# A three-stage attention and mixing kernel: weight ring in two parts, weight conversions moved into token mixing, two factors split

## The chip, the cores and the metric

One core of a Trainium2 chip. The metric is the device time of one execution in microseconds, the median of several runs. The names TensorE (PE, with its weight loads PEld), VectorE (DVE), ScalarE (ACT), GpSimd (POOL) and SyncE (SP) are used as in the profile.

## The reference, cut to what matters

Three layers on 4 batches of 576 positions and 512 features, all float32:

```python
# attention with feature maps (8 heads of 64), then
u = x + real(fft(fft(x, axis=1), axis=2))          # layer 1
u = u + relu(layernorm(u) @ w_ch1) @ w_ch2         # 512 -> 2048 -> 512
h = relu(u.transpose(0, 2, 1) @ w_tok1) @ w_tok2   # layer 2: 576 -> 256 -> 576
u = u + h.transpose(0, 2, 1)                       # token mixing
out = u + relu(u @ w_ch1) @ w_ch2                  # channel mixing: 512 -> 1536 -> 512
```

## The kernel before, in words

Every product of float32 matrices is made of three matmuls of rounded parts (high times high, high times low, low times high). A high part is a ScalarE cast, a low part the difference, on VectorE or GpSimd.

The last layer is what the change touches. *Token mixing* takes the batches in the order 2, 3, 0, 1. Per batch there are five steps: `c_tr` transposes 128 positions on TensorE, ScalarE casts the result (`yth`, L1060), VectorE subtracts (`ytl`, L1061), and `c_tok1` multiplies (L1074 to L1076). Then come `hh` and `hl` (L1081, L1082), `c_tok2` (L1094) in two halves of four sums, and VectorE adds these to `u` (L1100).

*Channel mixing* is 24 units (p, b): six slices p of the hidden width for batches 2 and 3 in turn, then for 0 and 1. A unit multiplies 2 by 2 blocks with seven products in place of eight, twice: seven first products of 6 matmuls (L876) from the prepared factors `x` of `x_prep` (L845 to L852) into the banks X, Y, Z, and seven second products of 6 matmuls (L885), from the factors `g` of `part` (L911, low part through `later`, whose line is L1319). Their inputs are the four `relu` results and sums of these (`sums1` L919, L920; `sums2` L926). Factors 5 and 7 are made as a pair, and 6 and 4 as a pair. `flush` adds each finished sum to `u` (L940); in a batch's last unit it writes `outT` instead (L935, stores L938 on SP's queue). Second products of a unit run beside first products of the next.

The weights of channel mixing are needed as rounded parts of the seven factors. `w_seven` makes one quarter of those of a slice (p, which, s): raw words come in (L624), `words2` makes floats of them (ScalarE L509, VectorE L512, L513, L515, some microseconds later), GpSimd makes four sums of blocks (L644), ScalarE the high part (L652), GpSimd the low part in two pieces (L656), and both go to a scratch in DRAM (L663). `wa_plain` does the same for the token weights. `w_load` brings the parts of one slice back (L676, `ring`, three slots of 1792 KB), one load for the first products and one for the second of every pair of units.

The order of the work is written out by hand: `at(t, fn)` and `later(dt, fn)` put a call into a heap ordered by a planned time, and instructions are emitted in that order; each engine and each queue runs its instructions in order. `te` is the planned end of layer 1, `td` the planned start of channel mixing (69 behind it), and a unit has TU = 11.15 of planned time:

```python
second_ = ((20, x1), (21, z7), (23, x6), (24, z4), (26, x5), (30, y2), (31, x3))   # in TU/14
late = ahead[18:24]                                   # six conversions
at(td - 16 + 15 * n, w_seven, p, which, s, True)      # n = 0 to 5, first operation 12 later
```

The other 27 conversions run in layer 1, one every 9.3.

Of the kernel before, what the change touches and what calls it, by code (L numbers as in the profile page):

```python
# [46 lines left out]
HB = 288  # L47
# [7 lines left out]
def mixer_kernel(ctx: ExitStack, tc: tile.TileContext, qT, kT, vt, wphi, w11, w12, wt1, wt2, w21, w22,  # L55
# [73 lines left out]
    def a_open():  # L129
        ones = st.tile([128, 128], F32, name="ones")  # L130
        nc.vector.memset(ones, 1.0 / D)
        T["ones"] = ones
        T["ones_r"] = st.tile([128, 128], F32R, name="ones_r")
# [9 lines left out]
        P["tmp"] = pool("tmp", 1, "right")  # L143
# [469 lines left out]
    def w_seven(p, which, s, late=False):  # L613
# [25 lines left out]
        def then(v):  # L639
            a11, a12, a22, a21 = (v[:, n * 128:(n + 1) * 128] for n in range(4))  # L640
            x = [N["x"][:, n * 128:(n + 1) * 128] for n in range(4)]
            for o, a, c, op in ((0, a21, a22, ALU.add), (1, x[0], a11, ALU.subtract), (2, a11, a21, ALU.subtract),
                                (3, a12, x[1], ALU.subtract)):
                nc.gpsimd.tensor_tensor(out=x[o], in0=a, in1=c, op=op)  # L644
# [26 lines left out]
    def w_load(which, p, v):  # L671
# [154 lines left out]
    WI = {1: 4, 2: 5, 4: 6, 5: 0, 6: 1, 7: 2, 3: 3}  # L826
# [37 lines left out]
    def unit(p, b, v, last, t0, tu, end=False):  # L864
# [5 lines left out]
        def prod(i, out, start, stop):  # L870
            w, x = W2[0, v], T["xx", b]
            need(("xx", b, XI[i]))
            k = 0
            for kk in range(2):
                for hw, hx in ((0, 0), (0, 1), (1, 0)):
                    nc.tensor.matmul(out, w[:, kk, hw, WI[i]], x[XI[i]][:, hx, kk], start=(start and k == 0),  # L876
                                     stop=(stop and k == 5), skip_group_check=(i != 2))
                    k += 1

        def prod2(i, o, start, stop):  # L880
            w, g = W2[1, v], G[i]
# [83 lines left out]
        def s_x3():  # L965
# [50 lines left out]
        def y2():  # L1016
            if not end:
                open_z("y")
                return second(2, "y", True, True, 0, 0)
            o = [pw()[:, 0:HB] for _ in range(2)]  # L1020
            prod2(2, o, True, True)
            for m in range(2):
                later(0.3, flush, o[m].unsqueeze(1), 0, 0, (m,))
# [11 lines left out]
    def c_open():  # L1035
# [10 lines left out]
        T["ytl"] = pc.tile([128, 4, 512], F32R, name="ytl")  # L1046
# [3 lines left out]
    def c_tr(b, kt):  # L1050
# [4 lines left out]
        h = P["cv"].tile([128, 512, 2], F32R, tag="raw", name="yth", bufs=2).rearrange("q c t -> q (c t)")[:, 0:512]  # L1055
        l = T["ytl"][:, kt % 4]
# [250 lines left out]
    for n, (_, p, which, s) in enumerate(late):  # L1307
        at(td - 16 + 15 * n, w_seven, p, which, s, True)
# [69 lines left out]
```

## Time and profile before

| what | value |
|---|---|
| median of 3 runs | 1083.12 us (1082.85 to 1086.86) |
| profiled execution | 1085.0 us |
| its span | 1083.3 us, mean granted clock 0.991 |
| TensorE busy | 1030.6 us (95%) |
| VectorE, ScalarE, GpSimd busy | 711.2, 442.2, 460.1 us |
| attention and layer 1 | 0 to 692.6 us |
| token mixing | 692.6 to 764.9 us |
| channel mixing | 764.9 to 1083.3 us |

The profile is of one execution. Its span begins with the first instruction and ends with the last; 1.7 us of the execution's time lie around it. Stages are told apart by the lines that TensorE works on. Line numbers are those of the kernel before; in the changed kernel the same lines stand 3 to 7 further down.

### The profile page before, as it was taken

Reading aid. Unit: us, or ns where it says so; the run is one execution under the profiler, and the core shown is the slowest. Engines: PE = TensorE matmul, PEld = TensorE weight load, DVE = VectorE, ACT = ScalarE, POOL = GpSimd, SP = SyncE. Lnnn points to the kernel's source line nnn. Section 1 sums busy time; section 2 is a strip of 40 time slices with the busy share of each in tenths; the row PEclk is TensorE's granted clock in tenths of the full one; section 3 lists DMA queues with packets and bytes.
Section 4 is the critical chain, followed back from the end, with each engine's and each line's share of the span. In section 5 each row is a group of like instructions: output and inputs, shape, how many; then the busy total and the mean of one; then the engine's idle time right before and its main releaser. Section 6 shows DMA issues by size and latency. Waiting matters only on the chain.

```text
span 1083.3 us, 19688 instructions
## 1 busy us (share of the span) xinstructions
PE 1030.6 (95%) x7596; PEld 951.3 (88%) x7596; DVE 711.2 (66%) x1265; ACT 442.2 (41%) x961; POOL 460.1 (42%) x451
## 2 busy tenths in 40 slices
PE   9999999999999989999999999999788899899996
PEld 9887787867899989999999999987788799799995
DVE  5799787999756786634676333354567677756666
ACT  5776556653223433322333121134444435444441
POOL 3464334322102344443444000045767758656551
PEclk9999999999999999999999999999999999999999
DMA  5575564462057543675733363800255544545332
GB/s 183 172 217 178 162 200 168 141 224 84 12 221 232 183 151 108 228 265 192 282 127 134 121 216 119 333 2 27 84 191 215 196 156 148 201 160 192 136 137 88
DMA packets 63785, 178.41 MB, mean 165 GB/s; under 512 B 8660, under 2 KB 30100, under 8 KB 57036
## 3 DMA queue, kind: packets, MB, share of 16 engines
q1 hardware_dynamic: 55628, 143.60, 38.6%
q10 hardware_dynamic: 8064, 33.56, 8.2%
q8 instruction: 60, 0.98, 0.4%
q14 instruction: 33, 0.27, 0.1%
HBM read 126.39 MB, written 48.31 MB: 161 GB/s over the span
## 4 chain that ended last, share of the span: by engine, by line
PE 56%; DVE 9%; POOL 5%; issue 3%; ACT 1%; DMA 1%; ACTq 0%; DVEq 0%; POOLq 0%
PE pw L790 16%; PE pz L885 9%; PE pw L876 8%; POOL g L1319 3%; PE pk L813 3%; PE pk L812 3%; PE pk L814 3%; PE pa L812 3%; PE pa L814 3%; PE pa L813 3%; PE pw L1094 1%; PE pa L1094 1%; DVE t L513 1%; PE pk L1075 1%; DVE t L512 1%
## 5 line engine op out<-in xcount | busy, mean ns | idle before, releaser
L790 PE MATMUL pw<-xh,w 128*128 128x288 f32 x896 | 197.5, 295 | 0.0
L885 PE MATMUL pz<-g,ring 128*128 128x288 f32 x1002 | 157.6, 301 | 19.5 <-POOL g L1319 9.8
L885 PEld LDWEIGHTS pz<-g,ring 128*128 128x128 f32 x1002 | 141.4, 191 | 25.9 <-POOL g L1319 14.5
L876 PE MATMUL pw<-x,ring 128*128 128x288 f32 x1008 | 153.4, 299 | 10.3 <-DVE f L898 5.4
L798 DVE SCALAR_TENSOR_TENSOR gl<-pw,gh 128x288 fp32r<-128x288 f32 x128 | 58.0, 454 | 148.8 <-ACT gh L797 148.5
L876 PEld LDWEIGHTS pw<-x,ring 128*128 128x128 f32 x1008 | 140.8, 190 | 13.2 <-DVE f L898 7.0
L790 PEld LDWEIGHTS pw<-xh,w 128*128 128x128 f32 x896 | 149.9, 188 | 1.2 <-issue 1.0
L940 DVE TENSOR_TENSOR u<-u,pz 128x576 f32<-128x576 f32 x152 | 113.9, 752 | 56.4 <-PE pz L885 52.9
L797 ACT ACTIVATE gh<-pw 128x288 fp32r<-128x288 f32 x128 | 52.6, 411 | 213.6 <-PE pw L790 211.8
L790 PE MATMUL pw<-xl,w 128*128 128x288 f32 x448 | 132.3, 295 | 0.5 <-POOL xl L773 0.5
L199 POOL TENSOR_TENSOR l<-raw,h 128x384 fp32r<-128x384 f32 x48 | 51.8, 1084 | 96.2 <-ACT h L195 83.7
L1319 POOL TENSOR_TENSOR g<-t,g 128x576 fp32r<-128x576 f32 x46 | 66.3, 1442 | 52.4 <-ACT g L911 49.6
L790 PEld LDWEIGHTS pw<-xl,w 128*128 128x128 f32 x448 | 84.1, 188 | 0.7 <-POOL xl L773 0.7
L812 PE MATMUL pk<-gh,w 128*128 128x288 f32 x256 | 76.4, 298 | 4.7 <-ACT gh L797 2.8
L813 PE MATMUL pk<-gl,w 128*128 128x288 f32 x256 | 76.8, 300 | 4.1 <-DVE gl L798 4.1
L812 PE MATMUL pa<-gh,w 128*128 128x288 f32 x256 | 75.9, 297 | 0.0
L814 PE MATMUL pk<-gh,w 128*128 128x288 f32 x256 | 75.8, 296 | 0.0
L814 PE MATMUL pa<-gh,w 128*128 128x288 f32 x256 | 75.6, 295 | 0.0
L813 PE MATMUL pa<-gl,w 128*128 128x288 f32 x256 | 75.4, 294 | 0.0
L1319 ACT ACTIVATE f<-f 128x288 f32<-128x288 f32 x72 | 32.0, 444 | 90.3 <-DVE f L898 90.1
L1319 POOL TENSOR_TENSOR g<-f,g 128x288 fp32r<-128x288 f32 x69 | 58.1, 856 | 20.4 <-ACT g L911 20.2
L259 PEld LDWEIGHTS pk<-v,ek 128*128 128x128 f32 x512 | 61.6, 192 | 5.8 <-issue 5.8
(205 smaller groups left out, 2385.0 us busy)
## 6 DMA issues: line engine op xcount, KB each, us to landing
ring<-wd SPq DMA_DIRECT2D x24, 1792.0 KB
w<-wd ACTq DMA_DIRECT2D x24, 1024.0 KB
raw<-in_w SPq DMA_DIRECT2D x32, 512.0 KB
wd<-wst SPq DMA_DIRECT2D x24, 448.0 KB
wd<-raw SPq DMA_DIRECT2D x24, 448.0 KB
wd<-wst SPq DMA_DIRECT2D x16, 512.0 KB
wd<-w ACTq DMA_DIRECT2D x32, 256.0 KB
raw<-in_w SPq DMA_DIRECT2D x48, 128.0 KB
```

The source lines that it names most:

```text
L199: nc.gpsimd.tensor_tensor(out=l, in0=src, in1=h, op=ALU.subtract)
L259: nc.tensor.matmul(T["kv", i][j][:, o:o + 65], e[:, (t % 2) * 2 + j, s, :], v[:, t - 1, j * 65:j * 65 + 65], start=False, stop=(u == 1 and ...
L790: nc.tensor.matmul(out, w[:, k, fs], x[:, k, :], start=(n == 0), stop=(n == 11))
L797: nc.scalar.activation(out=gh, in_=out, func=AF.Relu)
L798: nc.vector.scalar_tensor_tensor(out=gl, in0=out, scalar=0.0, in1=gh, op0=ALU.max, op1=ALU.subtract)
L812: nc.tensor.matmul(out, wh[:, f % 4, ds], gh, start=(f == f0), stop=False)
L813: nc.tensor.matmul(out, wh[:, f % 4, ds], gl, start=False, stop=False)
L814: nc.tensor.matmul(out, wl[:, f % 4, ds], gh, start=False, stop=last)
L876: nc.tensor.matmul(out, w[:, kk, hw, WI[i]], x[XI[i]][:, hx, kk], start=(start and k == 0), stop=(stop and k == 5), skip_group_check=(i != 2))
L885: nc.tensor.matmul(o[s], w[:, s, hw, WI[i]], g[hx], start=(start and k == 0), stop=(stop and k == 2), skip_group_check=(i != 2))
L940: nc.vector.tensor_tensor(out=u, in0=u, in1=o, op=ALU.add)
L1319: fn(*a, **k)
```

## The change

- `yth` gets four slots of its own in the pool of token mixing, where it shared two buffers `raw` with the conversions. `ones` and `ones_r` move to another pool.
- The four sums of a conversion are written to other slots, in an order that fits (L644). The parts of a slice lie in the order in which factors are used (`WI`).
- `w_load` makes two parts of every load: part 0 with the four factors that are used first, part 1 with the other three, in two DMAs as these lie at both ends of the row. Each part has three slots of its own and its own planned time.
- 24 conversions (15 of channel weights and the 9 of token weights, mixed) run in layer 1, one every 9.0. The last nine begin 36 before its planned end, one every 13: two meet the end of layer 1, five token mixing, two the first two units.
- The pair (6, 4) becomes two factors: 6 is made 3.4 after its last first product, 4 at the old place. The pair (5, 7) comes 0.2 earlier. Second products run in the order x1, z7, x6, x5, z4, x3, y2.
- In the last unit the sums of x go to two banks of the pool `pw`, flushed one by one, and y2 to a bank of `pz`.

```diff
     def w_load(which, p, v):   # now (which, p, v, part, eng)
-        t = P["r"].tile([128, 2, 2, 7, 128], F32R, tag="w", name="ring", bufs=3)
-        W2[which, v] = t
-        nc.sync.dma_start(out=t.bitcast(F32), in_=WD[1, which, p])
+        i0 = 2 - which
+        n = (4, 3)[part]
+        t = P["r"].tile([128, 2, 2, n, 128], F32R, tag="w%d" % part, name="ring", bufs=3)
+        src = WD[1, which, p]
+        for o, a, e in ((0, i0, i0 + 4),) if part == 0 else ((0, 0, i0), (i0, i0 + 4, 7)):
+            eng.dma_start(out=t[:, :, :, o:o + e - a].bitcast(F32), in_=src[:, :, :, a:e])
+            for k in range(a, e):
+                W2[which, v, k] = t[:, :, :, o + k - a]
...
-    WI = {1: 4, 2: 5, 4: 6, 5: 0, 6: 1, 7: 2, 3: 3}
+    WI = {3: 0, 5: 1, 6: 2, 7: 3, 1: 4, 2: 5, 4: 6}
...
-            ga = P["g"].tile([128, 2, n, HB], F32R, tag="g%d" % n, name="g", bufs=5 if n == 1 else 3)
+            ga = P["g"].tile([128, 2, n, HB], F32R, tag="g%d" % n, name="g", bufs=6 if n == 1 else 2)
...
-            later(2.2 if end else 2.8, lambda: part((5, 7), h["t13"], 2))
-            if end:
-                later(2.7, lambda: part(6, h["t24"][:, 0:1]))
+            later(2.2 if end else 2.6, lambda: part((5, 7), h["t13"], 2))
+            later(2.7 if end else 3.4, lambda: part(6, h["t24"][:, 0:1]))
...
-            later(4.2, lambda: part((6, 4), h["t24"], 2))
+            later(4.2, lambda: part(4, h["t24"][:, 1:2]))
...
         def open_x():
-            h["x"] = pz()
+            h["x"] = [pw()[:, 0:HB] for _ in range(2)] if end else pz()
...
             o = h[key]
+            if isinstance(o, list):
+                prod2(i, o, start, stop)
+                for m in range(2):
+                    later(0.3, flush, o[m].unsqueeze(1), row, hf, (m,))
+                return
...
-        second_ = ((20, x1), (21, z7), (23, x6), (24, z4), (26, x5), (30, y2), (31, x3))
+        second_ = ((20, x1), (21, z7), (23, x6), (26, x5), (28.2, z4), (30, x3), (31.5, y2))
...
-        h = P["cv"].tile([128, 512, 2], F32R, tag="raw", name="yth", bufs=2).rearrange("q c t -> q (c t)")[:, 0:512]
-        l = T["ytl"][:, kt % 4]
+        h, l = T["yth"][:, kt % 4], T["ytl"][:, kt % 4]
...
-    late = ahead[18:24]
-    del ahead[18:24]
-    tcv = tb2 - V('c2', 40)
+    sevens, plain = ahead[:24], ahead[24:]
+    lanes = [(plain if n % 8 in (2, 5, 7) else sevens).pop(0) for n in range(24)]
+    tcv = tb2 - V('c2', 38)
...
-        tcv += V('c4', 9.3)
+        tcv += V('c4', 9.0)
+    tcv = max(tcv, te - 36)
+    for kind, *a in sevens:
+        at(tcv, w_seven, *a, True)
+        tcv += 13
...
-                t = times1[n] - 2 * TU + (0.2 * TU + 0.5 if which == 0 else 1.1 * TU + 0.5)
-                at(tc_ + 0.3 + 0.01 * (2 * v + which) if 2 * v + which < 3 else t + TU, w_load, which, p, v)
+                for part, t in enumerate((-1.05, -0.65) if which == 0 else (-0.5, 0.1)):
...
+                        at(times1[n] + t * TU, w_load, which, p, v, part, nc.sync)
...
-    for n, (_, p, which, s) in enumerate(late):
-        at(td - 16 + 15 * n, w_seven, p, which, s, True)
```

VectorE at the start of token mixing, first before and then changed (`gl` and the sums from `pk`, `pa` are the end of layer 1; L1061, L1082 and L1100 are `ytl`, `hl` and the sums, L1064, L1085 and L1103 in the changed kernel):

```order
L1061 TENSOR_TENSOR ytl<-pw,yth 128x512
L817 TENSOR_TENSOR u<-u,pk 128x288 x2
L817 TENSOR_TENSOR u<-u,pa 128x288 x2
L1061 TENSOR_TENSOR ytl<-pw,yth 128x512 x2
L1061 TENSOR_TENSOR ytl<-pw,yth 64x512
L1082 SCALAR_TENSOR_TENSOR hl<-pk,hh 128x512 x2
L1061 TENSOR_TENSOR ytl<-pw,yth 128x512 x2
L1100 TENSOR_TENSOR u<-u,pw 128x288
```

```order
L1064 TENSOR_TENSOR ytl<-pw,yth 128x512
L822 TENSOR_TENSOR u<-u,pk 128x288 x2
L822 TENSOR_TENSOR u<-u,pa 128x288 x2
L512 TENSOR_SCALAR t<-t 128x512
L513 SCALAR_TENSOR_TENSOR t<-raw,t 128x512
L515 SCALAR_TENSOR_TENSOR t<-raw,t 128x512
L1064 TENSOR_TENSOR ytl<-pw,yth 128x512 x2
L1064 TENSOR_TENSOR ytl<-pw,yth 64x512
L1085 SCALAR_TENSOR_TENSOR hl<-pk,hh 128x512 x2
L1064 TENSOR_TENSOR ytl<-pw,yth 128x512 x2
L512 TENSOR_SCALAR t<-t 128x512
L513 SCALAR_TENSOR_TENSOR t<-raw,t 128x512
```

The bit operations of two conversions now stand among the first batch's and the second batch's operations; three more follow in the later batches.

GpSimd in unit 0, first before and then changed (`g<-t` of 576 columns is a low part of a pair, of 288 that of a single factor from the sums; L644 and L656 are a conversion):

```order
L1319 TENSOR_TENSOR g<-t,g 128x576
L926 TENSOR_TENSOR t<-f,t 128x288
L1319 TENSOR_TENSOR g<-f,g 128x288 x2
L644 TENSOR_TENSOR raw<-t 128x128
L644 TENSOR_TENSOR raw<-raw,t 128x128
L644 TENSOR_TENSOR raw<-t 128x128
L644 TENSOR_TENSOR raw<-t,raw 128x128
L1319 TENSOR_TENSOR g<-t,g 128x576
```

```order
L1326 TENSOR_TENSOR g<-t,g 128x576
L931 TENSOR_TENSOR t<-f,t 128x288
L1326 TENSOR_TENSOR g<-t,g 128x288
L1326 TENSOR_TENSOR g<-f,g 128x288 x2
L644 TENSOR_TENSOR raw<-t 128x128
L644 TENSOR_TENSOR raw<-raw,t 128x128
L644 TENSOR_TENSOR raw<-t 128x128
L644 TENSOR_TENSOR raw<-t,raw 128x128
L1326 TENSOR_TENSOR g<-t,g 128x288
```

The sixth factor's low part has moved ahead of the conversion's four sums; the fourth's stays behind them.

SyncE's queue where the output of batches 2 and 3 is stored, first before and then changed (`wd_5555` and `wd_5798` are the first-product weights of the pair of units that starts with unit 14):

```order
L676 DMA ring<-wd_4977 128x3584
L938 DMA outT<-t 128x288 x4
L676 DMA ring<-wd_5307 128x3584
L938 DMA outT<-t 128x288 x12
L676 DMA ring<-wd_5555 128x3584
```

```order
L679 DMA ring<-wd_5458 128x4x512
L943 DMA outT<-t 128x288 x4
L679 DMA ring<-wd_5458 128x4x128
L679 DMA ring<-wd_5458 128x4x256
L943 DMA outT<-t 128x288 x6
L679 DMA ring<-wd_5798 128x4x512
L943 DMA outT<-t 128x288 x6
L679 DMA ring<-wd_5798 128x4x256
L679 DMA ring<-wd_5798 128x4x128
```

Part 0 of the load now stands behind six of the twelve stores, part 1 behind all of them.

## Rows read from the trace of the kernel before

**Rows 1.** Windows by stage; columns: from:to, length, busy (count) per engine, clock, DMA share, GB/s.

```profile
692.60:764.90 72.30, 70.29 (x420) 60.25 (x419) 34.83 (x67) 25.04 (x44) 30.04 (x23) 0.98 0.20 76
764.90:790.00 25.10, 19.06 (x122) 17.65 (x122) 12.46 (x20) 10.48 (x25) 19.05 (x22) 0.93 0.26 95
790.00:890.00 100.00, 88.11 (x638) 84.99 (x637) 68.17 (x106) 44.29 (x105) 71.92 (x78) 1.00 0.54 192
890.00:949.80 59.80, 52.23 (x367) 50.23 (x366) 44.48 (x67) 29.78 (x66) 41.68 (x37) 0.97 0.51 182
949.80:1060.00 110.20, 110.04 (x811) 108.16 (x812) 69.78 (x114) 48.31 (x116) 67.68 (x67) 1.00 0.40 149
```

**Rows 2.** Waits of TensorE, 790 to 890 us.

```profile
PE pz L885 <- DVE u L940: 4.9, 3, 1.9
PE pz L885 <- POOL g L1319: 4.8, 5, 2.2
PE pw L876 <- ACT c L891: 1.2, 1, 1.2
PE pw L876 <- DVE f L898: 0.8, 1, 0.8
```

**Rows 3.** Groups by line, 764.9 to 949.8 us: conversion operations.

```profile
L656 POOL TENSOR_TENSOR raw<-raw,wst 128x512 f32<-128x512 f32 x6 | 7.7, 1285 | 0.7 <-ACT wst L652 0.7
...
L656 POOL TENSOR_TENSOR raw<-t,wst 128x384 f32<-128x384 f32 x6 | 6.1, 1010 | 0.0
...
L513 DVE SCALAR_TENSOR_TENSOR t<-raw,t 128x512 uint32<-128x512 uint32 x5 | 5.7, 1136 | 0.2
```

**Rows 4.** Timeline of VectorE, 757 to 766 us: a conversion beside idle GpSimd.

```profile
762.23 0.42 DVE L512 TENSOR_SCALAR t<-t 128x512 uint32<-128x512 uint32 x1
762.69 0.69 DVE L513 SCALAR_TENSOR_TENSOR t<-raw,t 128x512 uint32<-128x512 uint32 x1
763.41 0.69 DVE L515 SCALAR_TENSOR_TENSOR t<-raw,t 128x512 uint32<-128x512 uint32 x1
```

**Rows 5.** Timeline of all engines, 795 to 800 us.

```profile
795.62 1.26 DVE L512 TENSOR_SCALAR t<-t 128x512 uint32<-128x512 uint32 x1
...
799.05 1.06 PE L885 MATMUL pz<-g,ring 128*128 128x288 f32 x6 [1.47 <-DVE u L940]
```

**Rows 6.** Timeline of all engines, unit 0, 780 to 786 us.

```profile
782.23 1.40 POOL L1319 TENSOR_TENSOR g<-t,g 128x576 fp32r<-128x576 f32 x1
...
783.68 2.45 PE L885 MATMUL pz<-g,ring 128*128 128x288 f32 x11 [2.92 <-POOL g L1319]
```

**Rows 7.** Timeline of all engines, a steady unit, 989.5 to 993 us.

```profile
991.49 1.48 PEld L885 LDWEIGHTS pz<-g,ring 128*128 128x128 f32 x11 [0.26 <-POOL g L1319]
```

**Rows 8.** Timeline of ScalarE, token mixing, 688 to 766 us.

```profile
720.71 1.30 ACT L1081 ACTIVATE hh<-pk 128x512 fp32r<-128x512 f32 x2 [1.15 <-PE pk L1076]
...
736.64 1.30 ACT L1081 ACTIVATE hh<-pk 128x512 fp32r<-128x512 f32 x2 [1.72 <-PE pk L1076]
...
750.82 0.59 ACT L1060 CAST yth<-pw 128x512 fp32r<-128x512 f32 x1 [1.68 <-PE pk L1076]
...
755.76 1.29 ACT L1081 ACTIVATE hh<-pk 128x512 fp32r<-128x512 f32 x2 [1.53 <-PE pk L1076]
```

**Rows 9.** Timeline of GpSimd, token mixing, 685 to 766 us.

```profile
710.23 1.42 POOL L845 TENSOR_TENSOR xq<-u 128x576 f32<-128x576 f32 x1 [36.10 <-DVE u L1100]
```

**Rows 10.** Chain that ended last, 920 to 960 us: start, length, what.

```profile
940.77 8.97 DMA ring<-wd
```

**Rows 11.** Timeline of TensorE, 949 to 952 us.

```profile
949.78 1.87 PE L876 MATMUL pw<-x,ring 128*128 128x288 f32 x12 [2.91 <-DMA ring<-wd]
```

**Rows 12.** Page, part 3: DMA queues, packets, MB, share of sixteen engines.

```profile
q1 hardware_dynamic: 55628, 143.60, 38.6%
q10 hardware_dynamic: 8064, 33.56, 8.2%
```

**Rows 13.** Waits of TensorE, last unit, 1060 to 1083.3 us.

```profile
PE pz L885 <- DVE t L935: 3.3, 2, 2.4
```

More of the change, by code (lines that the diff above doesn't have):

```diff
@@ L129, in a_open @@
     def a_open():
-        ones = st.tile([128, 128], F32, name="ones")
+        P["tmp"] = pool("tmp", 1, "right")
+        ones = P["tmp"].tile([128, 128], F32, name="ones")
         nc.vector.memset(ones, 1.0 / D)
         T["ones"] = ones
-        T["ones_r"] = st.tile([128, 128], F32R, name="ones_r")
+        T["ones_r"] = P["tmp"].tile([128, 128], F32R, name="ones_r")
         nc.vector.tensor_copy(out=T["ones_r"], in_=ones)
@@ L641, in then @@
             x = [N["x"][:, n * 128:(n + 1) * 128] for n in range(4)]
[L642 to L643 removed]
+            for o, a, c, op in ((1, a21, a22, ALU.add), (2, x[1], a11, ALU.subtract), (3, a11, a21, ALU.subtract),
+                                (0, a12, x[2], ALU.subtract)):
                 nc.gpsimd.tensor_tensor(out=x[o], in0=a, in1=c, op=op)
@@ L669, in mixer_kernel, with w_load @@
     W2 = {}
-    def w_load(which, p, v):
+    def w_load(which, p, v, part, eng):
         need(*[("wd", ("w", 1, which, p, s)) for s in range(2)])
-        t = P["r"].tile([128, 2, 2, 7, 128], F32R, tag="w", name="ring", bufs=3)
-        W2[which, v] = t
-        nc.sync.dma_start(out=t.bitcast(F32), in_=WD[1, which, p])
+        i0 = 2 - which
[6 more added lines that the diff above has]
+                W2[which, v, k] = t[:, :, :, o + k - a]
     FIRST = [(1, 0), (1, 1), (2, 0)]
@@ L875, in prod @@
                 for hw, hx in ((0, 0), (0, 1), (1, 0)):
-                    nc.tensor.matmul(out, w[:, kk, hw, WI[i]], x[XI[i]][:, hx, kk], start=(start and k == 0),
+                    nc.tensor.matmul(out, w[:, kk, hw], x[XI[i]][:, hx, kk], start=(start and k == 0),
                                      stop=(stop and k == 5), skip_group_check=(i != 2))
@@ L884, in prod2 @@
                 for hw, hx in ((0, 0), (0, 1), (1, 0)):
-                    nc.tensor.matmul(o[s], w[:, s, hw, WI[i]], g[hx], start=(start and k == 0),
+                    nc.tensor.matmul(o[s], w[:, s, hw], g[hx], start=(start and k == 0),
                                      stop=(stop and k == 2), skip_group_check=(i != 2))
@@ L1016, in y2 @@
         def y2():
[L1017 to L1023, printed above, removed]
+            open_z("y")
+            second(2, "y", True, True, 0, 0)
         for k, fn in ((0, s_y2), (1, s_x1), (4, s_x6), (5, s_z7), (8, s_x5), (11, s_x3), (13, s_z4)):
             at(t0 + k * st_, fn)
-        second_ = ((20, x1), (21, z7), (23, x6), (24, z4), (26, x5), (30, y2), (31, x3))
+        second_ = ((20, x1), (21, z7), (23, x6), (26, x5), (28.2, z4), (30, x3), (31.5, y2))
         if end:
@@ L1045, in c_open @@
         T["wt"] = (*t1, *t2)
-        T["ytl"] = pc.tile([128, 4, 512], F32R, name="ytl")
+        T["yth"], T["ytl"] = (pc.tile([128, 4, 512], F32R, name="yt" + c) for c in "hl")
         U[1] = P["cu"].tile([128, 4, S], F32, name="u1")
@@ L1297, in mixer_kernel @@
             for which in range(2):
-                t = times1[n] - 2 * TU + (0.2 * TU + 0.5 if which == 0 else 1.1 * TU + 0.5)
-                at(tc_ + 0.3 + 0.01 * (2 * v + which) if 2 * v + which < 3 else t + TU, w_load, which, p, v)
+                for part, t in enumerate((-1.05, -0.65) if which == 0 else (-0.5, 0.1)):
+                    if 2 * v + which < 3:
+                        at(tc_ + 0.3 + 0.01 * (2 * v + which), w_load, which, p, v, part, nc.sync)
+                    else:
+                        at(times1[n] + t * TU, w_load, which, p, v, part, nc.sync)
         ps = [q for q, c in order1 if c == b]
```

9 lines of the change are left out of this document (4 added, 5 removed).

## The prediction

> **What bounds the kernel now.** I read the windows by stage first, then TensorE's waits, then single stretches of the timeline, the chain last. The windows [rows 1] give the measure: from 949.8 to 1060 TensorE does 811 matmuls in 110.20 us, 135.9 ns each at full clock; 84 matmuls make a unit, so a unit takes 11.4 us, and nothing but TensorE bounds it. At the same pace the 122 matmuls of 764.9 to 790 would take 16.6 us instead of 25.1, the 638 of 790 to 890 86.7 instead of 100.0, the 367 of 890 to 949.8 49.9 instead of 59.8. So units 0 to 15 lose 8.5 + 13.3 + 9.9 = 31.7 us against the later ones. TensorE's waits of 790 to 890 [rows 2] name who is late: VectorE's flush `u` and `f`, GpSimd's low parts `g`, and `c`. Both engines carry there what they don't carry later: weight conversions [rows 3].
>
> Two stretches show how a conversion reaches TensorE. At 795.62 the first of its three VectorE operations takes 1.26 us beside a GpSimd subtraction; a flush is queued behind the three, and TensorE waits 1.47 us for it [rows 5]. With GpSimd idle the three take 0.42 + 0.69 + 0.69 = 1.8 us [rows 4]. In unit 0 the low part of the pair (6, 4) starts on GpSimd only at 782.23, behind four subtractions of a conversion; TensorE waits 2.92 us for it [rows 6].
>
> **The change, part by part.** The sum is made against the profiled execution, 1085.0 us (span 1083.3 and 1.7 around it), 1.9 above the median 1083.1; the difference is applied to the median.
>
> 1. *Conversions out of units 2 to 9.* Six conversions had GpSimd work behind 764.9; the last four of them fell into units 2 to 9 and now run earlier. Each had four subtractions and two low parts of 1.29 and 1.01 us on GpSimd, and three VectorE operations, of which the middle one took 1.14 in the mean [rows 3]. The 13.3 us lost in 790 to 890 can go whole (upper bound). The lower bound is 5: the waits for `g`, 4.8 of the 11.7 us waited there [rows 2], and the smaller gaps may be the units' own. I take 11, near the upper end, because 949.8 to 1060 has the same units without conversions and loses none of this; 2.3 is left for the end of the conversion that still runs beside unit 1. **−11 (−13 to −5).**
>
> 2. *Units 0 and 1.* They keep two conversions, at nearly the same places. But the sixth factor's low part is now an instruction of its own, ahead of the four subtractions, so the 2.92 us at 783.68 goes [rows 6], and what half clock lies around that wait (the granted clock is 0.93 in that window [rows 1]: 25.1 × 0.07 = 1.7 us). Next late is the fourth factor's part, still behind the subtractions, but its product now stands four products later. **−3 (−4.6 to 0).**
>
> 3. *Ring in two parts.* In the chain TensorE waits for a load issued at 940.77 that takes 8.97 us [rows 10], behind twelve output stores on SP's queue, which themselves wait for VectorE's last sums. It costs TensorE 2.91 us [rows 11]. The first part now stands behind six of these stores and is 4/7 as large: of the landing alone some 8.97 × 3/7 = 3.8 us is gained, more than the 2.9 needed. The second part stands behind all twelve, but its first product comes some 4 us after the first part's, and it is 3/7 as large. **−2.9 (−2.9 to 0).** The 24 loads become 72 of shorter rows. From the two queues [rows 12] a packet of 2.58 KB holds an engine 0.386 × 16 × 1083.3 us / 55628 = 120 ns, one of 4.16 KB 176 ns: an estimate of 29 ns fixed and 0.035 per byte. Two whole loads, as a pair of units (22.9 us) needs them, then go from 9.9 to 13.6 us of sixteen engines, and the DMA share of a steady stretch from 0.40 [rows 1] to some 0.56. Covered by the unit ahead: 0; without that cover a late load would cost what this one did, 2.9.
>
> 4. *Sixth and fourth factor apart, second products in another order.* In a steady unit TensorE's weight load waits 0.26 us for the pair's low part [rows 7]; the sixth alone is half as long, so that goes, at most 14 × 0.26 = 3.6 us over the later units. In its place the second products of 6 and 5 now stand with one product between them, and the latter waits for the former's flush: some 0.2 again. GpSimd gets one instruction more per unit and ScalarE one; in 949.8 to 1060 they are busy 67.7 and 48.3 of 110.2 us [rows 1], which covers both. Units 10 to 13, where factor preparation fills GpSimd, should gain from the earlier sixth. **−1.5 (−3.6 to +3).**
>
> 5. *Token mixing takes five conversions.* What it gives back first: from one `hh` cast to the next a batch takes 15.93 us, the last one 19.12, since `yth` found one buffer and waited for the matmuls that read it [rows 8]. Its own four slots give back 3.2 us, and the clock (0.98 over 72.3 us [rows 1]) up to 1.4; I take 4. What it takes on: by hand, the conversion among the first batch's casts makes `yth` wait for GpSimd, 1.3; the next delays VectorE's sums, and so the banks of the second half, 1.5; the third does the same beside a busy GpSimd, 2; the last two 0.3 and 1. Together 6. From both sides: nothing, if all fits into the slack of the steps; or 13.3 / 4 = 3.3 each, what each cost among the units, 16.6 in all. I take 6, nearer the low end, as GpSimd is busy only 30.0 of 72.3 us here [rows 1]. **+2 (−4 to +13).**
>
> The Trainium skill ("SBUF — State Buffer", Who interferes with whom) states that a VectorE operation with two SBUF inputs, or one in a two-port mode, and a GpSimd operation that reads SBUF lock each other out for a whole instruction. The trace agrees: 1.26 us beside 0.42 for one operation [rows 4, 5]. By that rule alone, with all five conversions meeting GpSimd, an estimate would make this term some 5 us larger and the sum 1070; by the rows of 762 it is as taken.
>
> 6. *Last unit.* Two of its second products wait 3.3 us for VectorE sums that free their banks, one of them 2.4 [rows 13]. With x's sums in banks of the other pool that falls partly; VectorE's own queue is late next, and one sum of x's becomes two. **−2 (−3.3 to +2).**
>
> 7. Layer 1 keeps two late conversions at its end and the others at nearly the old pace: 0 (±1).
>
> Sum: −11 − 3 − 2.9 − 1.5 + 2 − 2 = −18.4: 1064.7, say **1065 us.**
>
> **The rivals.**
>
> A. *Conversions cost token mixing what they cost the units.* For: the instructions are the same, and queues run in order. Against: GpSimd is less busy. Term 5 is then +13, the time 1076.
>
> B. *Slower: ScalarE's cast of a conversion stands behind GpSimd's factor preparation.* GpSimd waits 36.1 us for batch 2's sums and then has six operations of 1.42 us, 8.5 us, queued [rows 9]. A conversion's subtractions behind such a block hold its ScalarE cast, behind that `yth`, and so TensorE. With 1.2 us of slack in a step a full block costs 7.3. It decides from (1088.5 − 1083.1 + 20.4 + 3.2) / 5 = 5.8 us for each of five conversions on; at 7.3 the time is 1083.1 − 20.4 − 3.2 + 36.5 = 1096. Against: the block starts at 710.23 and could be over by 718.8, before the `hh` cast of 720.71 [rows 8]; the conversion queued behind it comes with the third batch, after that cast.
>
> C. *The waits of units 0 to 9 are the units' own.* Terms 1 and 2 vanish: −4.4, 1079, no change that can be told. For: the waits name `g` and `u`, not conversions. Against: the later units, with the same instructions, don't lose it.
>
> **How the numbers follow.** Forecast 0.72, A 0.13, C 0.10, B 0.05. The bounds of terms 1 and 5 give the forecast alone some 1056 to 1074; with A and the edges I give 1054 to 1077, and B and C lie outside. A measurement of this kernel can tell about 0.5% (5.4 us) from no change. Faster (below 1077.7) holds the forecast and A: 0.85; the same holds C: 0.10; slower (above 1088.5) holds B: 0.05.
>
> **What would show it.** Right: in the stretch of units 2 to 9 of the changed kernel 638 matmuls take some 89 us and the waits name almost no `u`; no wait for the ring near the output stores; batches of token mixing of 16 to 18 us, none of 19. Wrong: batches of 19 us or more (A); `yth` held behind conversion casts for 6 us or more, with a granted clock well under 0.98 there (B); waits for `g` and `u` of some 10 us with no conversion near them (C); or a wait for the ring in steady units (term 3).

## The result, and the profile after

The changed kernel takes 1076.39 us (median; 1074.71 to 1078.27). Measured beside it on the same chips, the kernel before takes 1086.22. The ratio is 0.9916, with a 95% interval of 0.9894 to 0.9938: some 9 us faster. Forecast were 18 us, so the change went the way that was predicted and was worth half of it. The time lies at the upper edge of the range, and at what rival A gave (1076).

The profiled execution took 1078.27 us, its span 1076.5. I cut it where the first transposes, the first first-product of unit 0 and then 25, 100, 60 and 90 us have passed, as [rows 1] are cut for before (the last but one is 90 us here, 110.2 there). Windows by stage of the changed kernel (from:to, length, then busy time and count of PE, PEld, DVE, ACT, POOL, granted clock, DMA share, GB/s):

```profile
693.70:777.50 83.80, 76.00 (x418) 63.78 (x417) 43.56 (x79) 32.51 (x59) 51.79 (x53) 0.90 0.48 168
777.50:802.50 25.00, 21.31 (x141) 20.16 (x140) 15.55 (x25) 12.94 (x32) 19.98 (x24) 0.93 0.45 153
802.50:902.50 100.00, 99.74 (x730) 97.37 (x731) 67.83 (x109) 48.25 (x116) 65.78 (x74) 1.00 0.48 152
902.50:962.50 60.00, 54.40 (x371) 51.91 (x370) 45.12 (x66) 29.85 (x70) 40.67 (x39) 0.94 0.57 180
962.50:1052.50 90.00, 90.00 (x661) 87.97 (x660) 58.27 (x95) 41.64 (x101) 54.71 (x63) 1.00 0.48 153
1052.50:1076.50 24.00, 17.46 (x122) 16.09 (x120) 16.55 (x31) 5.61 (x13) 4.66 (x6) 0.95 0.30 99
```

Channel mixing does what was predicted. Units 2 to 9 do 730 matmuls in 100 us where [rows 1] have 638, units 0 and 1 141 in 25.0 us where they have 122 in 25.1. From its first matmul to the end channel mixing takes 299.0 us, before 318.4: 19.4 us gained, where terms 1 to 4 and 6 summed to 20.4. What TensorE waits for from 775 us on:

```profile
PE pw L881 <- DVE f L903: 5.1, 6, 2.0
PE pz L890 <- DVE t L940: 5.0, 5, 2.1
PE pw L890 <- DVE u L945: 0.9, 1, 0.9
PE pz L890 <- DVE u L945: 0.3, 1, 0.3
```

The waits for GpSimd's `g` of [rows 2] are gone, and of the 4.9 us for `u` in units 2 to 9 0.3 are left (the 0.9 is in the last unit).

Token mixing is where the rest went. It takes 83.8 us instead of 72.2, 11.6 more where term 5 had 2. The first transpose comes 1.0 later. 19.4 − 11.6 − 1.0 is the 6.8 us between the two spans. ScalarE's timeline in token mixing of the changed kernel answers to [rows 8]:

```profile
706.84 1.29 ACT L1084 ACTIVATE hh<-pk 128x512 fp32r<-128x512 f32 x2 [2.67 <-PE pk L1079]
...
721.27 0.62 ACT L652 CAST wst<-raw 128x512 fp32r<-128x512 f32 x1 [11.52 <-DMA wd<-wst]
...
722.21 1.06 ACT L1063 CAST yth<-pw 128x512 fp32r<-128x512 f32 x2
...
730.34 1.30 ACT L1084 ACTIVATE hh<-pk 128x512 fp32r<-128x512 f32 x2 [1.60 <-PE pk L1079]
...
746.97 1.29 ACT L1084 ACTIVATE hh<-pk 128x512 fp32r<-128x512 f32 x2 [1.69 <-PE pk L1079]
...
756.43 0.68 ACT L509 ACTIVATE t<-raw 128x512 f32<-128x512 f32 x1 [4.46 <-POOL raw L656]
...
757.57 0.58 ACT L1063 CAST yth<-pw 128x512 fp32r<-128x512 f32 x1
...
767.86 0.60 ACT L1084 ACTIVATE hh<-pk 128x512 fp32r<-128x512 f32 x1 [6.45 <-PE pk L1079]
```

From `hh` to `hh` the second batch takes 23.5 us (706.84 to 730.34), the third 16.6, the last 20.9, where [rows 8] had 15.93 and 19.12. In the second batch the high-part cast of a conversion (L652) stands at 721.27 ahead of `yth`, and before it ScalarE was idle for 11.52 us, waiting for the store of the high part of the conversion before, since there is one buffer (`wst`) for it. GpSimd's sums for this cast ended at 714.23, so some 4.5 us of this idle time are GpSimd's and 7.0 the store's:

```profile
713.77 0.46 POOL L644 TENSOR_TENSOR raw<-t,raw 128x128 f32<-128x128 f32 x1
```

Why the store was late, the chain (start, length, what) and SP's queue show:

```profile
711.96 9.24 DMA wd<-wst
721.27 1.03 ACT wst L652 x2
```

```profile
700.24 11.62 SPq L679 DMA_DIRECT2D ring<-wd  x9
711.96 1.88 SPq L663 DMA_DIRECT2D wd<-wst  x1
```

The first three ring loads, 5.4 MB in nine DMAs, are issued at the start of token mixing and fill SP's queue until 711.86. The store is issued behind them at 711.96 and lands 9.24 us later, at 721.2. The Trainium skill ("DMA: Bandwidth & Descriptors", Queues, rings and completion order) states that the DMAs that SP issues share one ring on each DMA engine and are taken from it in ring order. The trace agrees as far as it goes: from 700 to 722 us SP's queue (q1 in [rows 12]) kept the DMA engines busy for 94% of the time, and the store landed 9.24 us behind its issue. No run put the store on another queue, so ring order and mere sharing of the DMA engines are not told apart. In the last batch `yth` of 757.57 stands behind a conversion's first cast (756.43), which waited 4.46 us for GpSimd's low part of the conversion before. Behind that, VectorE holds `ytl` up:

```profile
759.49 1.80 DVE L513 SCALAR_TENSOR_TENSOR t<-raw,t 128x512 uint32<-128x512 uint32 x1
761.32 1.77 DVE L515 SCALAR_TENSOR_TENSOR t<-raw,t 128x512 uint32<-128x512 uint32 x1
763.01 1.27 DVE L1064 TENSOR_TENSOR ytl<-pw,yth 128x512 fp32r<-128x512 f32 x2
```

In sum TensorE waits 7.7 us in token mixing:

```profile
PE pk L1077 <- ACT yth L1063: 3.4, 2, 3.1
PE pk L1078 <- DVE ytl L1064: 2.9, 2, 2.7
PE pa L1097 <- DVE u L1103: 1.4, 2, 0.9
```

The 3.1 us for `yth` end at 722.84, in the second batch; the 2.7 us for `ytl` lie in the last. The sum is less than the 11.6. The rest is the clock: the granted clock of token mixing is 0.90, 0.98 in [rows 1]. TensorE ran at half clock behind the wait of the second batch, from some 723 to 729 us, and behind that of the last one, until 773.5 us, and at full clock from there. Three windows, columns as above:

```profile
723.70:725.70 2.00, 2.00 (x5) 1.52 (x6) 0.41 (x1) 0.15 (x1) 1.92 (x3) 0.50 0.92 327
...
769.70:771.70 2.00, 2.00 (x10) 2.00 (x10) 0.69 (x1) 2.00 (x5) 1.33 (x1) 0.50 0.00 0
...
773.70:775.70 2.00, 2.00 (x18) 2.00 (x17) 1.25 (x3) 1.24 (x2) 2.00 (x3) 1.00 0.45 179
```

### The profile page after: what moved, and what is told of

Same layout as the page of the kernel before. It is cut to its first block, busy times and chain, and to the rows that moved or that the text cites. A ratio compares the mean times of both kernels' runs of the same rounds, so it can differ in the third digit from the quotient of the medians.

```text
span 1076.5 us, 19868 instructions
## 1 busy us (share of the span) xinstructions
PE 1036.7 (96%) x7596; PEld 954.8 (89%) x7596; DVE 714.6 (66%) x1268; ACT 451.1 (42%) x987; POOL 463.6 (43%) x477
## 5 line engine op out<-in xcount | busy, mean ns | idle before, releaser
L881 PE MATMUL pw<-x,ring 128*128 128x288 f32 x1008 | 157.7, 300 | 5.1 <-DVE f L903 5.1
L890 PE MATMUL pz<-g,ring 128*128 128x288 f32 x984 | 155.4, 301 | 5.3 <-DVE t L940 5.0
L890 PEld LDWEIGHTS pz<-g,ring 128*128 128x128 f32 x984 | 139.1, 191 | 10.2 <-DVE t L940 5.4
L1326 POOL TENSOR_TENSOR g<-t,g 128x288 fp32r<-128x288 f32 (+1 forms) x69 | 71.2, 1032 | 43.2 <-ACT g L916 41.4
```

The lines of the kernel that those rows point to most:

```text
L881: nc.tensor.matmul(out, w[:, kk, hw], x[XI[i]][:, hx, kk], start=(start and k == 0), stop=(stop and k == 5), skip_group_check=(i != 2))
L890: nc.tensor.matmul(o[s], w[:, s, hw], g[hx], start=(start and k == 0), stop=(stop and k == 2), skip_group_check=(i != 2))
L1326: fn(*a, **k)
```

## The experiments

One table for all of them. "Token mixing" runs from the first transpose to the first first-product, with TensorE's busy time and the rest of it; "channel mixing" from there to the end of the span.

| kernel | time, us | ratio to before, 95% interval | first transpose at | token mixing = busy + rest | channel mixing |
|---|---|---|---|---|---|
| before | 1084 to 1086 | 1 | 692.7 | 72.2 = 70.2 + 2.0 | 318.4 |
| changed | 1076.4 | 0.9916 (0.9894 to 0.9938) | 693.7 | 83.8 = 76.0 + 7.8 | 299.0 |
| ring loads spread | 1071.5 | 0.9876 (0.9849 to 0.9903) | 693.6 | 76.2 = 71.4 + 4.8 | 299.0 |
| conversions as before | 1067.8 | 0.9840 (0.9815 to 0.9865) | 692.6 | 67.2 = 67.0 + 0.2 | 308.1 |
| before, `yth` slots alone | 1080.6 | 0.9963 (0.9948 to 0.9979) | 693.5 | 67.2 = 67.0 + 0.2 | 319.3 |
| 6 and 4 a pair again | 1080.7 | 0.9952 (0.9931 to 0.9972) | 693.9 | 83.1 = 73.3 + 9.8 | 301.7 |
| ring whole again | 1083.0 | 0.9986 (0.9969 to 1.0003) | 694.2 | 80.4 = 73.5 + 6.9 | 308.8 |
| last unit's banks as before | 1080.8 | 0.9968 (0.9953 to 0.9983) | 694.2 | 81.5 = 73.4 + 8.1 | 302.6 |
| 30 conversions in layer 1 | 1070.4 | 0.9865 (0.9846 to 0.9885) | 698.7 | 71.5 = 69.1 + 2.4 | 296.9 |
| the same, loads spread | 1072.3 | 0.9884 (0.9866 to 0.9902) | 702.0 | 72.4 = 69.2 + 3.2 | 296.8 |
| loads spread, preparation on VectorE | 1072.8 | 0.9892 (0.9870 to 0.9914) | 693.4 | 77.2 = 71.5 + 5.7 | 299.5 |
| loads spread, three conversions in units | 1068.9 | 0.9862 (0.9842 to 0.9882) | 693.7 | 71.0 = 68.5 + 2.5 | 301.2 |
| mixed placing, loads spread | 1066.3 | 0.9834 (0.9816 to 0.9852) | 692.5 | 70.4 = 68.1 + 2.3 | 301.7 |
| loads at once, later | 1071.2 | 0.9875 (0.9856 to 0.9894) | 695.7 | 76.2 = 71.4 + 4.8 | 298.8 |

### The initial ring loads spread

```diff
-                        at(tc_ + 0.3 + 0.01 * (2 * v + which), w_load, which, p, v, part, nc.sync)
+                        at(tc_ + 10 + 4.5 * (2 * (2 * v + which) + part), w_load, which, p, v, part, nc.sync)
```

> Only the nine initial ring loads of the changed kernel move: one every 4.5 us of planned time from 10 behind the start of token mixing, instead of all at once. Store theory: in the changed kernel the second batch of token mixing takes 23.5 us from cast hh to cast hh because a conversion's store waits on SP's queue and in the DMA engines behind these loads (5.4 MB), the one high-part buffer is not free, and ScalarE's cast of the next conversion waits 11.5 us ahead of yth. Then that wait goes, this batch falls to 16 to 17 us, and the time falls by about 7 to 1069; the last batch (20.9 us) stays as it is. Work theory (the conversions' own operations hold up the engines): the batch stays above 21 us and the time within 2 us of 1076.

Measured 1071.5 us, 4.9 less than the changed kernel; token mixing falls by 7.6 to 76.2. ScalarE's timeline of this kernel:

```profile
706.77 1.30 ACT L1084 ACTIVATE hh<-pk 128x512 fp32r<-128x512 f32 x2 [2.64 <-PE pk L1079]
...
714.20 0.62 ACT L652 CAST wst<-raw 128x512 fp32r<-128x512 f32 x1 [4.51 <-POOL raw L644]
...
723.82 1.28 ACT L1084 ACTIVATE hh<-pk 128x512 fp32r<-128x512 f32 x2 [0.48 <-PE pk L1079]
...
740.53 1.29 ACT L1084 ACTIVATE hh<-pk 128x512 fp32r<-128x512 f32 x2 [1.69 <-PE pk L1079]
...
761.08 0.60 ACT L1084 ACTIVATE hh<-pk 128x512 fp32r<-128x512 f32 x1 [6.11 <-PE pk L1079]
```

The second batch takes 17.05 us, and the cast that waited for the store until 721.27 comes at 714.20. It still waits 4.51 us there, for GpSimd's sums. The last batch stays at 20.5. The store theory held; a forecast of 7 us was somewhat high for the time by the medians, right for the stage.

### The conversions placed as before

```diff
-    sevens, plain = ahead[:24], ahead[24:]
-    lanes = [(plain if n % 8 in (2, 5, 7) else sevens).pop(0) for n in range(24)]
...
+    late = ahead[18:24]
+    del ahead[18:24]
+    tcv = tb2 - 40
...
+        tcv += 9.3
...
+    for n, (_, p, which, s) in enumerate(late):
+        at(td - 16 + 15 * n, w_seven, p, which, s, True)
```

> The changed kernel with the conversions placed as before the change (27 in layer 1, one every 9.3, the last six from 16 ahead of channel mixing, one every 15). If the conversions alone make both what units 2 to 9 gain and what token mixing loses: token mixing falls from 83.8 us to 68 to 72, channel mixing grows from 299 by 11 to 14, and the time is within 3 us of the changed kernel's 1076. If units 2 to 9 gain from the factors' and the ring's split instead: channel mixing grows by under 6, and the time is near 1068.

A miss that says most. Windows of token mixing and of units 2 to 9 of this kernel:

```profile
692.60:759.80 67.20, 67.01 (x419) 58.58 (x417) 34.85 (x67) 25.06 (x44) 30.18 (x23) 1.00 0.26 85
...
784.80:884.80 100.00, 92.88 (x660) 89.61 (x659) 71.89 (x111) 46.55 (x115) 74.16 (x89) 0.98 0.60 197
```

Channel mixing grows by 9.1 us, nearly all of it in units 2 to 9 (660 matmuls in 100 us against 730). Token mixing falls by 16.6 to 67.2, with the clock at 1.00. So the four conversions cost the units 9.1 us, 2.3 each, and the five cost token mixing 16.6, 3.3 each: their move alone loses some 7.5 us, and the changed kernel without it is the faster one, 1067.8 against 1076.4. The other parts of the change are worth 10.3 us of channel mixing (318.4 to 308.1). In units 2 to 9 of this kernel TensorE waits for VectorE's `f` (4.9 us) and `u` (2.3), and not for `g`. With the pair and without conversions there (two experiments on) the wait for `g` is 0.6 us. So the 4.8 us for `g` in [rows 2] took the pair and the conversions together.

### The slots of `yth` alone

```diff
-        h = P["cv"].tile([128, 512, 2], F32R, tag="raw", name="yth", bufs=2).rearrange("q c t -> q (c t)")[:, 0:512]
-        l = T["ytl"][:, kt % 4]
+        h, l = T["yth"][:, kt % 4], T["ytl"][:, kt % 4]
```

> The kernel before, with nothing but the four slots for yth (and the small move of ones that makes room for them). As predicted, the last batch of token mixing falls from 19.1 to 16 us and the kernel is 3 to 4.6 us faster than before. Rival: the last batch is late for the factor preparation on ScalarE and GpSimd, and nothing changes (within 1 us).

As expected: 3.9 us faster by the medians, token mixing 5.0 shorter. The window of token mixing of this kernel:

```profile
693.50:760.70 67.20, 67.01 (x418) 58.59 (x417) 34.82 (x67) 25.07 (x44) 30.14 (x23) 1.00 0.20 77
```

Token mixing with no more than the first steps of one conversion, at its end, is 67.2 us at full clock, with 67.01 of it busy. This is what the 83.8 us are to be measured against: 9.0 us more of busy time and 7.6 more of waiting. By batch (from the first transpose to the first `hh`, then from `hh` to `hh`) the 16.6 us are 1.1 in the first, 7.6 in the second, 0.8 in the third, 5.0 in the last and 2.1 behind the last `hh`.

These are figures of one execution. Two kernels of the table leave its token mixing as it is, those with 6 and 4 a pair again and with the last unit's banks as before: they took 83.1 and 81.5 us, with 6.3 and 6.4 us more of busy time and 9.6 and 7.9 more of the rest. So the conversions cost 14 to 17 us there, and how much of it is waiting and how much clock changes from one execution to the next.

### Factors 6 and 4 as a pair, second products in the old order

```diff
-            later(2.7 if end else 3.4, lambda: part(6, h["t24"][:, 0:1]))
+            if end:
+                later(2.7, lambda: part(6, h["t24"][:, 0:1]))
...
-            later(4.2, lambda: part(4, h["t24"][:, 1:2]))
+            later(4.2, lambda: part((6, 4), h["t24"], 2))
...
-        second_ = ((20, x1), (21, z7), (23, x6), (26, x5), (28.2, z4), (30, x3), (31.5, y2))
+        second_ = ((20, x1), (21, z7), (23, x6), (24, z4), (26, x5), (30, y2), (31, x3))
```

> The changed kernel with factors 6 and 4 made as a pair again and the second products in the old order; ring, conversions and last unit as changed. If the split is worth what was predicted, channel mixing is 1.5 us longer (0 to 4) than the changed kernel's 299.0, mostly in units 0 and 1 and 10 to 13; if the split carries units 0 to 9, channel mixing is longer by 6 or more; if it costs, it is shorter.

Channel mixing is 2.7 us longer, inside what was expected, but not as it was divided. Waits of TensorE for `g`, and windows of units 0 and 1, of the factor preparation and of the end:

```profile
PE pz L890 <- POOL g L1327: 6.3, 6, 2.9
```

```profile
777.00:802.00 25.00, 18.58 (x121) 17.40 (x120) 13.88 (x23) 10.88 (x25) 18.49 (x22) 0.93 0.39 137
902.00:962.00 60.00, 54.07 (x393) 52.22 (x392) 46.40 (x69) 30.27 (x69) 42.55 (x38) 1.00 0.56 180
1052.00:1078.70 26.70, 18.77 (x122) 17.37 (x120) 17.70 (x31) 5.77 (x14) 5.35 (x5) 0.90 0.27 89
```

Units 0 and 1 do 121 matmuls in 25 us again instead of 141, 2.7 us at 135.9 ns: that is term 2, with the 2.9 us wait for `g` back. In the 60 us that hold factor preparation the pair does 393 matmuls where the split does 371, so there the split costs 3.0: with the pair TensorE waits 2.9 us for `g` and 1.0 for the output sums `t` there, with the split 4.2 for `t` alone. At the end the pair takes 26.7 us for 122 matmuls where the split takes 24.0. The last unit itself makes 6 and 4 apart in both kernels, so this gain comes from the unit ahead of it or from the factors' buffers, which the edit also puts back; which, no run tells. In steady units (661 in 90 us in both) it does nothing.

### The ring in whole loads

```diff
-        for o, a, e in ((0, i0, i0 + 4),) if part == 0 else ((0, 0, i0), (i0, i0 + 4, 7)):
-            eng.dma_start(out=t[:, :, :, o:o + e - a].bitcast(F32), in_=src[:, :, :, a:e])
...
+        t = P["r"].tile([128, 2, 2, 7, 128], F32R, tag="w", name="ring", bufs=3)
+        eng.dma_start(out=t.bitcast(F32), in_=WD[1, which, p])
...
-                for part, t in enumerate((-1.05, -0.65) if which == 0 else (-0.5, 0.1)):
+                for part, t in enumerate((-0.755,) if which == 0 else (0.145,)):
```

> The changed kernel with whole ring loads (one DMA of 1792 KB, one slot of three for each), at the planned times of before. If splitting the ring is worth the wait it was meant for, the wait of some 2.9 us for the ring behind the output stores is back and channel mixing is 3 us longer than 299.0; if the first parts' earlier issue does nothing, it is within 0.5 us. The stall of the second batch of token mixing (23.5 us) stays in both cases, within 2 us, since the bytes ahead of the store are the same.

Channel mixing is 9.8 us longer, three times what was expected. The window that holds the output stores, and the wait in it:

```profile
899.60:959.60 60.00, 50.60 (x322) 48.23 (x321) 40.05 (x58) 26.27 (x61) 36.98 (x35) 0.89 0.47 162
```

```profile
948.60 1.81 PE L877 MATMUL pw<-x,ring 128*128 128x288 f32 x6 [3.39 <-DMA ring<-wd]
```

322 matmuls in 60 us instead of 371 make 6.7 of the 9.8. Of these the wait is 3.39 us, near the 2.91 of [rows 11], and the granted clock of the window, 0.89 instead of 0.94, is another 3 us. What a late load costs behind the wait itself was not in the prediction. Whole loads also cost 1.4 us in units 2 to 9 and 1.6 in the steady 90 us; TensorE waits for the ring there too, 0.5 and 0.8 us, and the rest stays open. The second batch of token mixing took 20.8 us, with a cast that waited 9.80 us for the store: the stall stayed, though 2.7 us shorter and so outside the 2 us expected.

### The last unit's banks as before

```diff
-            h["x"] = [pw()[:, 0:HB] for _ in range(2)] if end else pz()
+            h["x"] = pz()
...
+            if not end:
+                open_z("y")
+                return second(2, "y", True, True, 0, 0)
+            o = [pw()[:, 0:HB] for _ in range(2)]
```

> The changed kernel with the last unit's banks as before (x's sums in one bank pair of the second pool, y2 in two banks of the first). As predicted, the part from the last first product to the end is 2 us longer (0 to 3.3); if the banks cost nothing, it is within 0.5 us of the changed kernel's 15.8 us.

The end (the last 122 matmuls) takes 27.6 us instead of 24.0. Waits of TensorE there:

```profile
PE pz L890 <- DVE t L940: 3.3, 4, 0.9
PE pz L890 <- DVE u L945: 0.8, 1, 0.8
```

4.1 us of waits, near the 3.3 of [rows 13]; in the changed kernel 1.9 are left. The banks are worth 3.6, a little more than the upper bound of term 6.

### More conversions in layer 1

```diff
-    lanes = [(plain if n % 8 in (2, 5, 7) else sevens).pop(0) for n in range(24)]
-    tcv = tb2 - V('c2', 38)
+    lanes = [(plain if plain and n % 8 in (2, 5, 7) else sevens).pop(0) for n in range(30)]
+    tcv = tb2 - V('c2', 60)
```

> The changed kernel with the conversions earlier: 30 in layer 1 (from 60 ahead of its second part instead of 38, one every 9.0), three at its end, so that one touches token mixing and none channel mixing; everything else as changed, the nine ring loads at once too. If conversions cost token mixing 16.6 us and layer 1 nearly nothing, as the runs so far say (67.2 us without, 83.8 with), token mixing falls to 67 to 69 us, units 0 and 1 gain some 2 us, channel mixing is 297 to 299, and the time is 1060 to 1064. If a conversion costs the same wherever it stands (some 2.3 to 3.3 us), layer 1 grows by 12 or more and the time stays at 1072 to 1078.

Neither: 1070.4. Channel mixing falls to 296.9, and all batches but the first to 15.85 us; but layer 1 ends 5.0 us later, and the first batch is 4.3 us longer than without conversions. With the initial loads spread as well:

> 30 conversions in layer 1 and three at its end, as in the kernel that took 1070.4, and the ring loads spread as well. There the first batch of token mixing took 4.3 us longer (hh 16.35 us behind the first transpose, 12.0 without conversions). If this is again the one conversion whose casts stand behind the ring loads, the first batch falls to 12 to 13.5 us, and the time to 1066 to 1068.

A miss: 1072.3. The first batch is still late, and not for the ring. ScalarE's timeline of this kernel:

```profile
711.50 0.66 ACT L509 ACTIVATE t<-raw 128x512 f32<-128x512 f32 x1 [3.77 <-DMA raw<-in_w]
...
719.17 1.29 ACT L1084 ACTIVATE hh<-pk 128x512 fp32r<-128x512 f32 x2 [1.82 <-PE pk L1079]
```

A conversion's first cast, ahead of two `yth`, waits for its raw words to come in. Layer 1 ended at 702.0, 3.3 later than in the kernel beside it, though only token mixing's loads differ; this stays open. (In the kernel with the loads at once, but later, it ended 2.0 later than in the changed one, without a cause that I found.)

### Factor preparation on VectorE

```diff
-    x_prep(2, 0, td - 44, lambda k: td - 42.5 + 1.4 * k, 1.6, "d0123456")
-    x_prep(3, 1, td - 22, lambda k: td - 21 + 1.6 * k, 1.6, "d0123456")
+    x_prep(2, 0, td - 44, lambda k: td - 42.5 + 1.4 * k, 1.6, "d016")
+    x_prep(3, 1, td - 22, lambda k: td - 21 + 1.6 * k, 1.6, "d016")
```

> The kernel with the ring loads spread (1071.5), and in it four of the seven low parts of each factor preparation in token mixing go from GpSimd to VectorE (8 operations in all). Queue theory: the last batch is late (20.5 us) because ScalarE's first cast of a conversion waits 4.5 us for the conversion before on GpSimd, where preparation stands ahead of it, with yth behind that cast; then the batch falls to 16 to 18 us and the time by 2 to 4. Rival: VectorE, with its bit operations of 1.8 us, is the bound there, and the batch grows or stays above 20.

The last batch stays at 20.5 us, as the rival said, but the run doesn't decide between the two: ScalarE's cast still waits as long for GpSimd, since the three preparation operations ahead of the low part that it waits for all stayed there. That cast, and VectorE's timeline:

```profile
750.12 0.68 ACT L509 ACTIVATE t<-raw 128x512 f32<-128x512 f32 x1 [4.45 <-POOL raw L656]
```

```profile
753.19 1.80 DVE L513 SCALAR_TENSOR_TENSOR t<-raw,t 128x512 uint32<-128x512 uint32 x1
755.03 1.77 DVE L515 SCALAR_TENSOR_TENSOR t<-raw,t 128x512 uint32<-128x512 uint32 x1
756.72 0.74 DVE L857 TENSOR_TENSOR x<-xq,x 128x576 fp32r<-128x576 f32 x1
```

The bit operations stay long, and preparation is now queued behind them, ahead of `ytl`. That a VectorE operation with two SBUF inputs contends with a GpSimd operation that reads SBUF is the rule of the Trainium skill that term 5 weighed ("SBUF — State Buffer", Who interferes with whom), and the trace agrees: 1.80 and 1.77 us beside a GpSimd that works without a break, 0.69 in [rows 4]. By the estimate that the prediction made from this rule term 5 would have come to +7, still short of 11.6.

### Three conversions in units 0 to 2

```diff
-    for kind, *a in sevens:
-        at(tcv, w_seven, *a, True)
+    for n, (kind, *a) in enumerate(sevens):
+        at(tcv if n < 6 else te + 53 + 15 * (n - 6), w_seven, *a, True)
```

> The kernel with the ring loads spread (1071.5), and in it the last three conversions moved out of token mixing's last batch into units 0 to 2 (their first cast is 4 us of planned time ahead of channel mixing, then every 15). If the first cast of a conversion ahead of yth in ScalarE's order (waiting 4.5 us for GpSimd) and its bit operations ahead of ytl (4.1 us) are what makes the last batch 20.5 us long, the batch falls to 16 us and token mixing from 76.2 to 70.5 us or less; channel mixing then carries one conversion more, 1 to 3 us. Time 1067 to 1070. If the batch is late for factor preparation alone, it stays above 19.

As expected: the last batch 16.5 us, token mixing 71.0, channel mixing 301.2 (2.2 more, for one conversion), 1068.9 us. One conversion in the last batch cost 5 us, the four left in token mixing cost 3.8 together. Factor preparation alone does not make the batch late. Whether the cast's wait or the bit operations ahead of `ytl` weigh more is open, since both left with the conversion.

### A mixed placing

```diff
-        at(td - 16 + 15 * n, w_seven, p, which, s, True)
+        at((te - 10, te + 3, te + 16, td - 16, td - 1, td + 14)[n], w_seven, p, which, s, True)
```

This is the kernel with the conversions as before, with the ring loads spread and the last six placed by what the runs had shown.

> The changed kernel with 27 conversions in layer 1 as before the change, then one at its end, two in the first two batches of token mixing, three in units 0 to 2, and the ring loads spread. With some 1 us for a conversion in the first three batches (what the kernel with the ring loads spread shows) and 2.3 in a unit: token mixing 69 to 70.5 us, channel mixing 301 to 303, time 1064 to 1067. If layer 1 has no room for one more, it starts token mixing later than 694.5.

1066.3 us, the least of all, though its interval and that of the conversions as before (1067.8) overlap. Windows of token mixing and of units 2 to 9:

```profile
692.50:762.90 70.40, 68.10 (x418) 58.68 (x417) 39.72 (x76) 29.62 (x53) 42.06 (x41) 1.00 0.44 147
787.90:887.90 100.00, 97.75 (x715) 95.16 (x714) 68.08 (x109) 47.89 (x117) 67.85 (x78) 1.00 0.50 161
```

Units 2 to 9 do 715 matmuls in 100 us, where one conversion is left. Token mixing is 3.2 us longer than without conversions. Three have their casts in it, not two, as the one planned for the end of layer 1 reached ScalarE 1.9 us behind the first transpose: 1.1 us each. TensorE's longest wait there is 0.9 us, and the granted clock stays at 1.00.

### The loads at once, but later

```diff
-                        at(tc_ + 0.3 + 0.01 * (2 * v + which), w_load, which, p, v, part, nc.sync)
+                        at(tc_ + 26.3 + 0.01 * (2 * v + which), w_load, which, p, v, part, nc.sync)
```

> The changed kernel with all nine initial ring loads at once again, but 26 us of planned time later, just ahead of the store of the third conversion of token mixing instead of the first. Store theory: the stall follows the loads. The second batch, 23.5 us in the changed kernel, takes 17 as with the loads spread; ScalarE's next high-part cast, in the last batch, waits for the store (DMA wd<-wst) for 4 us or more, and the last batch takes 22 to 26 us instead of 20.5; token mixing 78 to 83 us. If what counts is only that the loads run while the first batches do (transfers against matmuls), token mixing is as with the loads spread, 76 us, and no cast waits for a store.

A miss: 1071.2, as with the loads spread, and no cast waits for a store. SP's queue, and ScalarE's cast that follows:

```profile
723.18 11.67 SPq L679 DMA_DIRECT2D ring<-wd  x9
734.95 1.27 SPq L663 DMA_DIRECT2D wd<-wst  x1
```

```profile
745.42 0.63 ACT L652 CAST wst<-raw 128x512 fp32r<-128x512 f32 x1
```

The store is again issued behind 11.67 us of loads, but the next high-part cast is due only at 745.42, 10.5 us behind it, when GpSimd's sums for it are done. In the changed kernel the sums were done 2.3 us behind the issue of the store and 7.0 ahead of its landing. So nine loads at once cost nothing as such; they cost where a store behind them is what the next cast waits for. That the one buffer carries the wait is what the trace names; a kernel with two buffers was not tried, so this is argued and not shown.

## Why the prediction was wrong

- **Term 1** (conversions out of units 2 to 9, −11): right, somewhat high. Putting them back costs 9.1 us. Rival C, that these waits are the units' own, is out, though `g` alone does not return with them.
- **Term 2** (units 0 and 1, −3): right, 2.7 us, by the split of the pair.
- **Term 3** (ring, −2.9): the mechanism was right, the size too small. Whole loads in the changed kernel cost 9.8 us, because half clock follows the wait, and for a part that stays open. The estimate of the DMA share in steady units, 0.56, was too high: 0.48 from 962.5 to 1052.5 us.
- **Term 4** (−1.5): in sum near 0 beside term 2: 3.0 lost with factor preparation, where a gain was expected, 2.7 gained at the end, nothing in steady units.
- **Term 6** (last unit, −2): the mechanism was right, the gain 3.6.
- **Term 7** (layer 1, 0 ± 1): +1.0.
- **Term 5** (token mixing, +2): this is the step that failed. The slots of `yth` gave back 5.0 where I took 4. The conversions took 16.6 where "by hand … together 6" stood. The hand count had waits alone, none over 2 us. The longest of TensorE's waits, 3.1 us in the second batch, was not in it: a store on SP's queue behind ring loads that stand at their old planned time but now meet a conversion. The last batch, counted at 1 us or so, was 5.0 longer. And the count had no clock at all: most of the 9.0 us of busy time is the same matmuls at half clock after these waits. For units 0 and 1 I counted that clock, for token mixing I took it only as something to be given back.

Rival A gave 1076 and 3.3 us for each conversion and got both, by luck: its reason (the same operations cost the same anywhere) is not what the runs show: a conversion costs some 1 us in the first three batches once the ring loads are out of its way, 5 in the last one, 2.3 in a unit. Rival B had the right form, `yth` held by a conversion's cast in ScalarE's order, with the wrong thing in front of it in the second batch (a store, not GpSimd) and the right one in the last (GpSimd behind factor preparation, 4.46 us). Both of their signs came, batches of over 19 us and `yth` held behind a conversion's cast with a granted clock of 0.90. The sum of all other terms was −20.4 against 19.4 gained in channel mixing. That they match so well is luck too: taken out one at a time, the parts are worth 9.1, 2.7, 9.8 and 3.6, 25.2 together, so they overlap and cannot be added up.

## What to carry to other kernels

When work moves from one stage to another, write down for the new place each thing that its instructions wait for, stores and free buffers included, and what stands ahead of those on their own queue. Where a matmul stream that has no slack is made to wait, price the wait with the half clock that follows it: here it added 6 to 9 us to some 8 to 10 us of waiting. And time the parts of a change apart: this one held a loss of 7.5 us inside a gain of 9.

## What the runs showed of the hardware

Nine loads of 256 to 1024 KB in a row kept SP's queue for 11.62 us, 1.3 each, where three raw loads of 128 to 256 KB take 1.28 together, and a store of 448 KB behind them took 9.24 us to land. And TensorE lost about as much to half clock after its waits in token mixing as to the waits themselves: 9.0 us of additional busy time beside 7.6 us of waiting in the profiled execution, 6.3 and 6.4 beside 9.6 and 7.9 in two others. With a longest wait of 0.9 us, in the mixed placing, the granted clock stayed at 1.00.
